# A fused attention and mixture-of-experts kernel: SyncE's registers choose the tiles' rows in place of VectorE's tables

## The chip, the cores and the metric

The kernel runs on one core of a Trainium2 chip. The metric is the device time of one execution in microseconds; the median of several runs counts, and less is better. The engines are called as the profile calls them: PE is TensorE, DVE is VectorE, ACT is ScalarE, POOL is GpSimd and SP is SyncE, which here issues nearly all plain transfers.

## The reference

There are 8 x 3584 = 28,672 tokens of 192 numbers. The first half is a causal convolution of seven taps with weights of its own for each token and each of eight heads (a softmax over the taps); the second is a layer of eight experts, of which each token goes to one.

```python
w = softmax(weight_gen, axis=-1)                      # (B, S, 8 heads, 7 taps)
x = sum over k of w[b, s, h, k] * x_pad[b, s + k, h]  # 24 numbers to a head
logits = x @ w_gate                                   # 8 experts
e_idx = argmax(logits); gate_w = softmax(logits)[e_idx]
eom = sigmoid(x @ w_output_gate)[e_idx]
out = gate_w * eom * (relu(x @ w1[e_idx]) @ w2[e_idx])   # 192 -> 1024 -> 192
```

## The kernel before

**Units.** The tokens are worked in 32 units of 896 (128 partitions by seven). For each unit VectorE and GpSimd make the softmax and the seven products (`softmax_steps`, L544; `tap_steps`, L577); in the first seven units TensorE adds the products in PSUM, later VectorE does (`acc_steps`, L612). `sum_steps` (L680) writes the sum as two 16-bit halves into a tile `rt`; seven DMA transposes, issued by SyncE, turn it (`gt`), and TensorE makes the gate logits. VectorE finds each token's expert and a running count; two small matmuls (L762) give, for each expert, the tokens on the partitions before and the unit's total. `place_steps` (L835) turns them into a row number for each token, and GpSimd scatters the tokens with seven indirect DMAs (`srtd<-rt,posi`) into `srtd`, a tensor in HBM in which each expert has a region of 2^15 rows. The total becomes the next unit's `base`.

**Tiles.** The expert layer works on tiles of T = 512, 384, 256 or 128 rows of one expert. `plan_rounds` (L27) fixes ahead, for each unit, how many tiles of which size follow it: enough rows are held back (`HOLD`, six times T) that some expert always has T rows ready. There are 76 tiles: ten small ones after units 2, 4 and 5 to start with, two more after unit 6, then one or two of 512 a unit, and 23 after the last one. Which expert and which rows a tile takes is known only on the chip. `tile_load` (L1003) reads both into SyncE's registers and issues the tile's loads: the rows' tokens and weights (`meta`), the rows themselves, transposed (`xT`), and the expert's weights in two halves (`wa`, `wb`). `gemm1_unit` and `gemm2_group` (L1018, L1040) are the two matrix products, 40 and 24 matmuls a group of 128 rows; between them ScalarE makes `hh`, the upper half of relu, and VectorE `hl`, the lower, and the PSUM bank is free when `hl` is done (L1038).

**The table.** `round_table` (L878) chooses on VectorE. For a round of R tiles of T rows it compares what each expert has with what the next tiles need, sums up over experts (a scan, L906), and forms from the sums the first row of each tile: `ti[1]` holds the rows, `ti[0]` the experts (a shift by 15, L925). It takes some eight VectorE instructions on one partition, of 8 or 16 elements in most rounds. `tile_load` reads two numbers of it for a tile (`value_load`, L1005 and L1006: a load from SBUF, and a test of its range). The last unit's table is followed by a dozen instructions that count what remains (L949 to L967); a loop behind the 76 tiles would work it off.

**The order of the work.** All engines' instructions stand in one order that a planner makes while the program is built (`Order`, L76): steps are generators, each engine has a clock of modelled costs, and the step that can start earliest goes next; ties go by rank. Each engine carries out its own instructions strictly in that order. A tile's first loads wait for the scatters that `state["writers"]` names (`scattered`, `loaded`, L390 to L403): all that stand ahead of the load in the program. SyncE's instructions (loads, transposes, register loads) stand in one row too, and one that waits holds up those behind it. At most two tiles are loaded ahead of TensorE (`AHEAD`), four after the last unit.

Of the kernel before, what the change touches and what calls it, by code (L numbers as in the profile page):

```python
# [17 lines left out]
P = 128  # L18
W = 194
WW = 3585  # L20
RMAX = 24
SHIFT = 15
NE = 8
# [32 lines left out]
def constants():  # L56

    ident = np.eye(P, dtype=np.float32)
    upper = np.triu(np.ones((P, P), np.float32), 1)
    r = np.arange(RMAX, dtype=np.float32)  # L60
    rr = np.tile(r[:, None], (1, 9))
    need = [T * r for T in (128, 256, 384, 512)]
    e8 = np.arange(8, dtype=np.float32) - 8.0
    flat = np.concatenate([rr.ravel(), *need, e8]).astype(np.float32)
    return np.concatenate([ident, upper, np.tile(flat[None], (P, 1))], axis=1)
# [41 lines left out]
class Queue:  # L107
# [110 lines left out]
def kernel(ctx: ExitStack, tc: tile.TileContext, x, wg, wgate, wogate, w1, w2, cst, out):  # L218
# [69 lines left out]
    f_mx = few[:, 80:136]  # L288
    f_lim = few[0:1, 189:190]

    f_next = few[0:1, 136:152].rearrange("p (e r) -> p e r", r=2)
    f_z = few[0:1, 152:170].rearrange("p (e r) -> p e r", r=2)
    f_done = f_next[:, :, 0]
    f_ex = ps[:, 2536:2538].bitcast(I32)
    f_rr = ps[0:1, 2512 : 2512 + RMAX]

    rest_free = [(0.0, 3904), (0.0, 1344)]
    mx_free, few_free, sq_free = [0.0], [0.0], [0.0]
# [44 lines left out]
    cf = cp.tile([P, cst.shape[1]], F32, name="cf")  # L343
    nc.scalar.dma_start(out=cf, in_=cst)
# [14 lines left out]
    o = 256  # L359
    rr = cf[0:1, o : o + RMAX * 9].rearrange("p (a b) -> p a b", b=9)  # L360
    o += RMAX * 9
    need = {}
    for k in (128, 256, 384, 512):
        need[k] = cf[0:1, o : o + RMAX]
        o += RMAX
    nc.vector.tensor_copy(f_e8, cf[:, o : o + 8])
# [3 lines left out]
    for e in range(NE):  # L370
        nc.vector.memset(base[:, e : e + 1], float(e * CAP - 1))
        nc.vector.memset(f_done[:, e : e + 1], float(e * CAP))


    cs = cp.tile([1, 1 + 8 * RMAX], F32, name="cs")
    nc.vector.memset(cs[:, 0:1], 0.0)
    nc.vector.memset(f_z[:, 8, :], float(DUMMY))
    nc.vector.tensor_copy(f_rr, rr[:, :, 0])
# [9 lines left out]
    state = {"base": base, "writers": [], "t": 0, "weights": 0, "rounds": 0}  # L388

# [154 lines left out]
    def softmax_steps(u):  # L544

        w4 = wloads[u]
        mxb = f_mx.unsqueeze(2).broadcast_to([P, NV, K])
        yield from take(mx_free, V)
# [21 lines left out]
        mx_free.append(od.cur.t)  # L570
# [109 lines left out]
    def sum_steps(u):  # L680
# [84 lines left out]
        od.add(place_steps(u), (RANK_C, u, 0), V)  # L765

# [67 lines left out]

    def place_steps(u):  # L835
# [11 lines left out]
        d["rk_home"].append((od.cur.t, d["rk_at"]))  # L847
        d["ranked"] = True
        if u in plan:
            od.add(round_steps(u), (RANK_R, u), V)  # L850
        else:
            state["rounds"] += 1
# [20 lines left out]
        d["sent"] = True  # L873
        d["sent_t"] = od.cur.t + 2.5
        rt_free.append((d["sent_t"], d["ri"]))


    def round_table(r, T, R, tail, bs):  # L878

        nm = f"{r}"  # L880
        rT = need[T][:, 0:R].unsqueeze(1).broadcast_to([1, 8, R])
        if R > 2:
            n = R
            nx = sp.tile([1, 8, RMAX], F32, tag="nx", bufs=1, name=f"nx{nm}")[:, :, 0:R]
            z = sp.tile([1, 9, RMAX], F32, tag="z", bufs=1, name=f"z{nm}")[:, :, 0:R]
            V.memset(z[:, 8, :], float(DUMMY))
            V.tensor_tensor(out=nx, in0=f_done.unsqueeze(2).broadcast_to([1, 8, R]), in1=rT, op=ALU.add)
            state["step"] = None
            yield V
        else:  # L890
            if state.get("step") != T:
                state["step"] = T if R == 2 else None
                if R == 2:
                    V.tensor_scalar(f_next[:, :, 1], f_done, float(T), None, op0=ALU.add)
                    yield V
            n = 2 if state["step"] == T else 1
            nx, z = f_next[:, :, 0:n], f_z[:, :, 0:n]

        gg = sp.tile([1, 8 * RMAX], F32, tag="gg", bufs=1, name=f"gg{nm}")[:, 0 : 8 * R]
        V.scalar_tensor_tensor(out=gg.rearrange("p (e r) -> p e r", r=R), in0=bs[0:1, :].unsqueeze(2).broadcast_to([1, 8, R]), scalar=0.0 if tail else 1.0 - T, in1=nx[:, :, 0:R], op0=ALU.add, op1=ALU.is_ge)  # L900
        yield V

        if state.get("limit") != R:
            V.memset(f_lim, float(R))
            state["limit"] = R
        V.tensor_tensor_scan(out=cs[:, 1 : 1 + 8 * R], data0=gg, data1=f_lim.broadcast_to([1, 8 * R]), initial=0.0, op0=ALU.add, op1=ALU.min)  # L906
        yield V
        cx = cs[:, 0 : 1 + 8 * R : R]

        V.scalar_tensor_tensor(out=z[:, 0:8, :], in0=cx[:, 0:8].unsqueeze(2).broadcast_to([1, 8, n]), scalar=-float(T), in1=nx, op0=ALU.mult, op1=ALU.add)  # L910
        ge = sp.tile([1, RMAX, 9], F32, tag="ge", bufs=1, name=f"ge{nm}")[:, 0:R, :]
        V.tensor_tensor(out=ge, in0=cx.unsqueeze(1).broadcast_to([1, R, 9]), in1=f_rr[:, 0:R].unsqueeze(2).broadcast_to([1, R, 9]), op=ALU.is_le)
        yield V
        n = 1 if R > 2 else n
        V.scalar_tensor_tensor(out=f_next[:, :, 0:n], in0=cx[:, 1:9].unsqueeze(2).broadcast_to([1, 8, n]), scalar=float(T), in1=z[:, 0:8, 0:n], op0=ALU.mult, op1=ALU.add)
        V.tensor_tensor(out=ge, in0=ge, in1=z[:, :, 0:R].rearrange("p e r -> p r e"), op=ALU.mult)
        yield V
        if R > 8:
            ti = sp.tile([1, 2, RMAX], I32, tag="til", bufs=1, name=f"ti{nm}")
        else:  # L920
            ti = sp.tile([1, 2, 8], I32, tag="ti", bufs=NU // 2 + 6, name=f"ti{nm}")
        with nc.allow_low_precision(reason="whole numbers"):
            V.tensor_reduce(out=ti[:, 1, 0:R], in_=ge, axis=AX, op=ALU.max)
        yield V
        V.tensor_scalar(ti[:, 0, 0:R], ti[:, 1, 0:R], SHIFT, None, op0=ALU.arith_shift_right)  # L925
        yield V
        return ti
# [3 lines left out]
    def round_steps(u):  # L931

        found, bs = [], U[u]["base"]
        yield V, lambda: state["rounds"] == u
        for k, (T, R) in enumerate(plan[u]):
            tail = u == NU - 1 and k == len(plan[u]) - 1
            pads = None
            if tail:
                pads = sp.tile([1, NE], I32, tag="bi", name="bi")
                bf = sp.tile([1, NE], F32, tag="bf", name="bf")  # L940
                V.tensor_scalar(bf, bs[0:1, :], 1.0, None, op0=ALU.add)
                yield V
                V.tensor_copy(pads, bf)
            ti = yield from round_table(f"{u}_{k}", T, R, tail, bs)
            for i in range(R):
                found.append((T, ti, i, pads if i == 0 else None))
        if u == NU - 1:

            more = sp.tile([1, NE], F32, tag="more", bufs=1, name="more")  # L949
            state["done"] = cp.tile([1, NE], F32, name="done")  # L950
            V.tensor_copy(state["done"], f_done)
            V.tensor_tensor(out=more, in0=bs[0:1, :], in1=f_done, op=ALU.subtract)
            yield V
            V.tensor_scalar(more, more, 128.0, None, op0=ALU.add)
            yield V
            morei = sp.tile([1, NE], I32, tag="morei", bufs=1, name="morei")
            V.tensor_copy(morei, more)
            yield V
            V.tensor_scalar(morei, morei, 7, None, op0=ALU.arith_shift_right)
            yield V  # L960
            V.tensor_copy(more, morei)
            yield V
            left = sp.tile([1, 1], F32, tag="left", bufs=1, name="left")
            V.tensor_reduce(out=left, in_=more, axis=AX, op=ALU.add)
            yield V
            lefti = state["left"] = sp.tile([1, 1], I32, tag="lefti", bufs=1, name="lefti")
            V.tensor_copy(lefti, left)  # L967
        state["rounds"] += 1
        yield SP, has(u, "sent")
        queue.extend((*f, max(od.cur.t, U[u]["sent_t"])) for f in found)  # L970
        if u == NU - 1:
            state["all"] = True
            queue[:] = mixed(queue)
# [8 lines left out]
    def tile_steps():  # L982

        while "all" not in state or queue:
# [4 lines left out]
            T, ti, i, pads, ready = queue.pop(0)  # L989
# [3 lines left out]
            if pads is not None:  # L993
                for e in range(NE):
# [308 lines left out]
```

## Time and profile before

| | us |
|---|---|
| median of 3 runs | 1228.21 |
| lowest and highest run | 1226.5, 1228.29 |
| the profiled execution's own time | 1230.08 |
| its span, first to last instruction | 1228.0 |

| engine | busy us | share of the span |
|---|---|---|
| TensorE, matmuls | 1132.9 | 92% |
| VectorE | 956.4 | 78% |
| GpSimd | 879.8 | 72% |
| ScalarE | 594.5 | 48% |

The shares are means over stretches that differ: the experts' weights are split into halves first, then units and tiles go side by side until the last unit, and the rest is tiles alone. Every instruction that the planner places bears the line of its helper (L151, or L125 for SyncE's and GpSimd's queues), so a row is known by its tiles. "x <- y" names what is written and what is read. In a row of waits stand the engine, what it was about to write, what it waited for, the total in us, how many times, and the longest. Waits belong to instructions in order: an engine that waits may hold back something else that was ready.

### The profile page before, as it was taken

To read this page: it belongs to the slowest core of one execution; us is meant where nothing else is said; L and a number is where in the kernel's file an instruction comes from. 1 tells how busy PE (TensorE), PEld (TensorE's weight loads), DVE (VectorE), ACT (ScalarE), POOL (GpSimd) and SP (SyncE) were. 2 spreads that over 40 slices of the span, in tenths; PEclk is the share of its full clock that TensorE was granted. 3 is DMA by queue.
4 is the path that set the end of the run, shared out by engine and by line. 5 is a ranking of instruction groups with operands and counts; after the bars stand their busy time and mean duration, and the time that the engine had idled before them with its cause. 6 is when DMAs were issued, how large, how long until landed. Compare 5 with 4: busy or idle time off the path is not lost.

```text
span 1228.0 us, 27900 instructions
## 1 busy us (share of the span) xinstructions
PE 1132.9 (92%) x9710; PEld 821.3 (67%) x9710; DVE 956.4 (78%) x2027; ACT 594.5 (48%) x1263; POOL 879.8 (72%) x778
## 2 busy tenths in 40 slices
PE   5988779899999999899999999899998999999997
PEld 2444448677666666676766666676666777988987
DVE  6898759899999898998998999899998663333331
ACT  3875345455555445454544454445544544344342
POOL 5668786668888788888888988888887663322222
PEclk9998989899999999999999999999999999999999
DMA  9998378999989869698769759997777679889992
GB/s 281 284 283 288 131 237 196 262 277 250 247 232 240 206 182 248 150 262 211 213 191 229 208 154 244 231 234 188 207 203 185 178 219 278 235 255 330 272 310 80
DMA packets 278047, 279.73 MB, mean 228 GB/s; under 512 B 211479, under 2 KB 236808, under 8 KB 277905
## 3 DMA queue, kind: packets, MB, share of 16 engines
q1 hardware_dynamic: 256016, 233.35, 69.1%
q0 software_dynamic: 21744, 44.30, 13.3%
q8 instruction: 76, 1.25, 0.4%
q14 instruction: 67, 0.54, 0.1%
q10 hardware_dynamic: 144, 0.29, 0.1%
HBM read 177.07 MB, written 60.87 MB: 194 GB/s over the span
## 4 chain that ended last, share of the span: by engine, by line
PE 40%; DVE 26%; POOL 12%; issue 8%; DMA 7%; SPq 3%; ACT 3%; POOLq 0%; DVEq 0%; ACTq 0%
PE ps L151 40%; DVE ps L151 11%; POOL gap L151 6%; DVE hl L151 5%; POOL srtd L151 3%; SPq L125 3%; DMA srtd<-rt,posi 2%; POOL out_dram L151 2%; DMA wa<-wd 2%; DVE rt L151 2%; DMA gt<-rt 1%; DVE vap L151 1%; ACT rt L151 1%; DVE ti L151 1%; DVE vt L151 1%
## 5 line engine op out<-in xcount | busy, mean ns | idle before, releaser
L151 PE MATMUL ps<-xT,wa 128*128 128x512 f16 (+3 forms) x2440 | 493.0, 350 | 42.7 <-DVE hl L151 33.3
L151 PE MATMUL ps<-wb,hh 128*128 128x192 f16 x3664 | 478.9, 248 | 4.8 <-DVE hl L151 4.8
L151 PE MATMUL ps<-wb,hl 128*128 128x192 f16 x1832 | 454.1, 248 | 0.1
L151 DVE SCALAR_TENSOR_TENSOR hl<-ps,hh 128x512 f16<-128x512 f32 (+1 forms) x472 | 307.5, 665 | 156.3 <-ACT hh L151 155.9
L151 POOL TENSOR_TENSOR gap<-x,w 128x960 f32<-128x960 f32 (+5 forms) x268 | 360.0, 1368 | 37.1 <-DVE lz L151 9.2
L151 ACT ACTIVATE hh<-ps 128x512 f16<-128x512 f32 (+1 forms) x472 | 272.1, 582 | 226.1 <-PE ps L151 223.5
L151 PEld LDWEIGHTS <-wa 128*128 128x128 f16 x2440 | 226.5, 99 | 226.7 <-issue 48.8
L151 PEld LDWEIGHTS <-hh 128*128 128x128 f16 x3664 | 337.0, 99 | 50.5 <-issue 9.4
L151 POOL DMA_INDIRECT out_dram<-ys,meta x216 | 214.5, 993 | 193.6 <-ACT ys L151 146.3
L151 POOL DMA_INDIRECT srtd<-rt,posi x224 | 229.0, 1022 | 87.0 <-issue 56.4
L151 DVE TENSOR_TENSOR ps<-ps,gap 128x1344 f32<-128x1344 f32 x125 | 194.2, 1554 | 21.8 <-POOL gap L151 21.8
L151 ACT ACTIVATE ys<-ps,sc 128x192 f32<-128x192 f32 x229 | 96.3, 421 | 221.0 <-PE ps L151 160.5
L151 PEld LDWEIGHTS <-hl 128*128 128x128 f16 x1832 | 180.9, 99 | 0.6 <-DVE hl L151 0.3
L151 PE MATMUL ps<-gap,cf 128*128 128x512 f32 x168 | 72.9, 569 | 3.2 <-DVE vap L151 3.2
L151 PE MATMUL ps<-vap,cf 128*128 128x512 f32 (+1 forms) x126 | 58.2, 603 | 13.5 <-DVE vap L151 12.9
L151 POOL TENSOR_TENSOR gap<-halo,w 128x1152 f32<-128x1152 f32 (+4 forms) x38 | 60.4, 1589 | 13.2 <-issue 5.7
L151 DVE SCALAR_TENSOR_TENSOR rt<-ps,sx,rt 128x448 f16<-128x448 f32 x64 | 57.9, 908 | 10.4 <-ACT rt L151 5.8
L151 PE MATMUL ps<-xT,late 128*128 128x128 f16 (+2 forms) x600 | 56.6, 251 | 0.0
L151 ACT ACTIVATE rt<-ps 128x1344 bf16<-128x1344 f32 x32 | 41.3, 1291 | 28.2 <-issue 18.3
L151 PEld LDWEIGHTS ps<-gap,cf 128*128 128x128 f32 x168 | 31.4, 199 | 34.8 <-issue 25.6
L151 PEld LDWEIGHTS ps<-vap,cf 128*128 128x128 f32 x126 | 24.9, 208 | 38.7 <-issue 22.9
L151 ACT ACTIVATE rt<-ps,sx 128x1344 f16<-128x1344 f32 x32 | 44.2, 1380 | 9.6 <-DVE isx L151 7.6
(123 smaller groups left out, 841.8 us busy)
## 6 DMA issues: line engine op xcount, KB each, us to landing
wb<-wd SPq DMA_DIRECT2D x76, 768.5 KB
wa<-wd SPq DMA_DIRECT2D x61, 768.0 KB
x<-in_x_dram SPq DMA_DIRECT2D x32, 672.0 KB
late<-wd SPq DMA_DIRECT2D x15, 768.0 KB
wa<-wd SPq DMA_DIRECT2D x61, 128.0 KB
w<-in_wg_dram SPq DMA_DIRECT2D x32, 196.0 KB
wd<-wpb SPq DMA_DIRECT2D x8, 768.5 KB
st<-in_w_dram SPq DMA_DIRECT2D x8, 768.0 KB
```

Source lines behind the costliest of these rows:

```text
L125: r = f(*args, **kwargs)
L151: r = f(*args, **kwargs)
```

## The change

The expert and row of a tile are chosen by SyncE's own register arithmetic.

- Each expert has a register `key`: what it has ready, times 2^11, plus its next free row divided by 128. ScalarE copies a unit's eight totals from PSUM into SBUF as whole numbers times 2^11 (`count_steps`); SyncE loads all eight in one load and adds them to the keys (`counted`).
- `pick` takes the largest key, or an unused row if none has T rows, and moves that key on: a start, eight maxima, three operations for each expert, and a mask. That is 34 register operations a tile. `tile_load` takes expert and row from the result; it loads nothing from SBUF.
- A unit's choices are made when its counts have come, ahead of its scatters; its tiles go into the queue when the scatters are issued, as before.
- With each unit the list of the scatters so far is kept (`writers`), and a tile's loads wait for its own unit's list.
- The last unit's pad rows are written when it is chosen for (`end_of`), and the number of leftover turns is made in registers and fetched from a constant table (`turns_left`).
- The softmax has two sets of words in PSUM (`mx_free`) where it had one.
- The constants' transfer shrinks from 576 columns to 264. The tables' VectorE instructions are gone.

The core of the diff:

```diff
-    mx_free, few_free, sq_free = [0.0], [0.0], [0.0]
+    mx_free, few_free, sq_free = [(0.0, 80), (0.0, 136)], [0.0], [0.0]
...
+    def spend(self, us):
+
+        self.issued = max(self.issued, self.order.now) + us
...
-    nc.scalar.dma_start(out=cf, in_=cst)
+    nc.scalar.dma_start(out=cf, in_=cst[:, 0:264])
...
+    def counted(cnt):
+
+        R.reg_load(came, cnt[0:1, 0:NE])
+        for e in range(NE):
+            R.reg_alu(key[e], key[e], came[e], ALU.add)
+        SP.spend(0.6)
+
+    def pick(T):
+
+        R.reg_mov(best, (T - 1 << HAVE) + (DUMMY >> ROW))
+        for e in range(NE):
+            R.reg_alu(best, best, key[e], ALU.max)
+        for e in range(NE):
+            R.reg_alu(came[e], key[e], best, ALU.is_ge)
+            R.reg_alu(came[e], came[e], (T >> ROW) - (T << HAVE), ALU.mult)
+            R.reg_alu(key[e], key[e], came[e], ALU.add)
+        R.reg_alu(best, best, low, ALU.bitwise_and)
+        SP.spend(1.1)
+        return R.snap(best, min_val=0, max_val=DUMMY >> ROW)
+
+    def end_of(e):
+
+        R.reg_alu(hit, key[e], HAVE, ALU.arith_shift_right)
+        R.reg_alu(best, key[e], low, ALU.bitwise_and)
+        R.reg_alu(best, best, 1 << ROW, ALU.mult)
+        R.reg_alu(best, best, hit, ALU.add)
+        row = R.snap(best, min_val=0, max_val=DUMMY - P)
+        scattered(SP.dma_start(out=srtd[bass.ds(row, P), :], in_=pad))
+        R.reg_alu(key[e], key[e], P - 1 << HAVE, ALU.add)
...
+    def count_steps(u):
+
+        cnt = U[u]["cnt"] = sp.tile([1, NE], I32, tag="cnt", bufs=CNT, name=f"cnt{u}")
+        S.activation(cnt, U[u]["rk"][0:1, 8:16], AF.Copy, scale=float(1 << HAVE))
...
+        d["writers"] = list(state["writers"])
...
-    def round_table(r, T, R, tail, bs):
...
     def round_steps(u):
 
-        found, bs = [], U[u]["base"]
-        yield V, lambda: state["rounds"] == u
...
+        yield SP, lambda: state["rounds"] == u and "counted" in U[u]
+        od.cur.t = max(od.cur.t, U[u]["counted"])
+        yield SP
+        counted(U[u]["cnt"])
+        found, subs = [], [(T, k) for k, (T, n) in enumerate(plan.get(u, ())) for _ in range(n)]
+        for T, k in subs:
+            if u == NU - 1 and k == len(plan[u]) - 1 and "ended" not in state:
+                state["ended"] = True
+                for e in range(NE):
+                    yield SP
+                    end_of(e)
+                    od.cur.t = od.now
+            yield SP
+            found.append((T, pick(T), u))
+        state["rounds"] += 1
...
-            d = tile_load(state["t"], T, ti, i, list(state["writers"]), ka, kb)
+            d = tile_load(state["t"], T, at, U[u]["writers"], ka, kb)
...
-    def tile_load(t, T, ti, i, writers, ka, kb):
+    def tile_load(t, T, at, writers, ka, kb):
         Gn = T // P
-        e = SP.value_load(ti[0:1, 0, i : i + 1], min_val=0, max_val=NE - 1)
-        row = SP.value_load(ti[0:1, 1, i : i + 1], min_val=0, max_val=DUMMY + 4 * P - T)
+        R.reg_alu(hit, at, SHIFT - ROW, ALU.logical_shift_right)
+        e = R.snap(hit, min_val=0, max_val=NE - 1)
+        row = at * (1 << ROW)
```

More of the change, by code (lines that the diff above doesn't have):

```diff
@@ L59, in constants @@
     upper = np.triu(np.ones((P, P), np.float32), 1)
-    r = np.arange(RMAX, dtype=np.float32)
-    rr = np.tile(r[:, None], (1, 9))
-    need = [T * r for T in (128, 256, 384, 512)]
     e8 = np.arange(8, dtype=np.float32) - 8.0
-    flat = np.concatenate([rr.ravel(), *need, e8]).astype(np.float32)
+    turns = np.arange(TURNS, dtype=np.int32).view(np.float32)
+    flat = np.concatenate([e8, turns])
     return np.concatenate([ident, upper, np.tile(flat[None], (P, 1))], axis=1)
@@ L371 @@
         nc.vector.memset(base[:, e : e + 1], float(e * CAP - 1))
[L372 to L378, printed above, removed]
+    R = nc.sync
+    key = [R.alloc_register(f"key{e}") for e in range(NE)]
+    came = [R.alloc_register(f"came{e}") for e in range(NE)]
+    best, hit = R.alloc_register("best"), R.alloc_register("hit")
+    for e in range(NE):
+        R.reg_mov(key[e], e << SHIFT - ROW)
     pad = cp.tile([P, W], I32, name="pad")
@@ L873, in place_steps @@
         d["sent"] = True
+        d["writers"] = list(state["writers"])
         d["sent_t"] = od.cur.t + 2.5
         rt_free.append((d["sent_t"], d["ri"]))
-    def round_table(r, T, R, tail, bs):
[L880 to L927, printed above, removed]
@@ L929 @@
     queue = []
     def round_steps(u):
-        found, bs = [], U[u]["base"]
-        yield V, lambda: state["rounds"] == u
[L935 to L946, printed above, removed]
@@ L947, in round_steps @@
-        if u == NU - 1:
[L949 to L967, printed above, removed]
@@ L988, in tile_steps @@
             _, kb = yield from take(wb_free, SP)
-            T, ti, i, pads, ready = queue.pop(0)
+            T, at, u, ready = queue.pop(0)
             if ready > od.now:
@@ L992, in tile_steps @@
                 yield SP
-            if pads is not None:
-                for e in range(NE):
-                    row = SP.value_load(pads[0:1, e : e + 1], min_val=0, max_val=DUMMY - P)
-                    scattered(SP.dma_start(out=srtd[bass.ds(row, P), :], in_=pad))
-            d = tile_load(state["t"], T, ti, i, list(state["writers"]), ka, kb)
+            d = tile_load(state["t"], T, at, U[u]["writers"], ka, kb)
             d["ready"] = od.cur.t
@@ L1202 @@
     own.close()
-    left = nc.values_load(state["left"][0:1, 0:1], min_val=0, max_val=N // P + NE)
+    lefti = cp.tile([1, 1], F32, name="lefti")
+    nc.sync.dma_start(out=lefti, in_=cst[0:1, bass.ds(state["turns"] + 264, 1)])
+    left = nc.values_load(lefti.bitcast(I32)[0:1, 0:1], min_val=0, max_val=TURNS - 1)
     gps.close()
@@ L1209 @@
         _, more = wa_free.pop()
[L1210 to L1216 removed]
+        d = tile_load(state["t"], P, pick(P), [], more, "wb")
         state["t"] += 1
@@ L1280 @@
 GT = 1
+CNT = 4
 TR_U = 6
```

61 lines of the change are left out of this document (30 added, 31 removed).

## The prediction

> **What bounds the kernel now.** I read the page first, then the busy time in four stretches, then the waits of each engine in those stretches, and last the chain and the timelines around TensorE's longest gaps. From the page:
>
> ```profile
> span 1228.0 us, 27900 instructions
> ```
>
> ```profile
> PE 40%; DVE 26%; POOL 12%; issue 8%; DMA 7%; SPq 3%; ACT 3%; POOLq 0%; DVEq 0%; ACTq 0%
> ```
>
> The chain passes mostly through TensorE and VectorE, with little on the transfers and on SyncE (SPq). The four stretches (weights are split; the first tiles; units and tiles side by side; tiles alone) give busy time per engine:
>
> ```profile
> 0.00:175.00 175.00, 139.82 (x580) 72.11 (x581) 131.81 (x303) 98.43 (x165) 124.88 (x104) 0.95 0.81 251
> 175.00:250.00 75.00, 62.96 (x584) 52.44 (x583) 63.68 (x149) 36.84 (x87) 50.89 (x42) 0.87 0.92 235
> 250.00:963.00 713.00, 672.82 (x5817) 481.50 (x5815) 665.42 (x1385) 351.35 (x788) 612.83 (x537) 0.98 0.83 215
> 963.00:1228.00 265.00, 257.33 (x2734) 215.29 (x2733) 95.49 (x194) 107.83 (x225) 91.23 (x96) 1.00 0.84 244
> ```
>
> The columns behind the length are PE, PEld, DVE, ACT and POOL. After 963 us TensorE works off the queue of tiles with nothing in its way. So the end is set by TensorE's work, which the change leaves alone, plus TensorE's idle time before 963: 713 - 673 = 40 us in the third stretch and 75 - 63 = 12 us in the second. That idle time is what can be won or lost. What ends it, in the second stretch and shortly before it (140 to 250 us, first row) and in the third (other two):
>
> ```profile
> PE ps L151 <- DMA wa<-wd: 8.1, 2, 5.9
> ```
>
> ```profile
> PE ps L151 <- DVE hl L151: 34.4, 38, 2.6
> PE ps L151 <- DMA gt<-rt: 4.5, 9, 0.8
> ```
>
> (us in total, times, longest). TensorE waits for VectorE's hl, which frees its PSUM banks; for the transposes gt of the gate logits; and early for two weight loads. In the third stretch VectorE, GpSimd and SyncE wait in their turn:
>
> ```profile
> DVE ps L151 <- POOL gap L151: 21.8, 18, 2.4
> ```
>
> ```profile
> POOL srtd L151 <- issue: 43.6, 146, 0.3
> POOL out_dram L151 <- issue: 20.3, 95, 0.3
> ```
>
> ```profile
> SPq L125 <- DMA srtd<-rt,posi: 128.6, 34, 10.4
> SPq L125 <- DVE rt L151: 63.1, 13, 15.2
> ```
>
> GpSimd's 612.8 busy plus 63.9 of short pauses ahead of its indirect DMAs is 676.7 of 713 us, so the units come at GpSimd's pace; VectorE (665.4) is close behind. SyncE stands still 128.6 us for scatters into the sorted rows.
>
> **The change part by part.**
>
> *VectorE's tables go.* The third stretch has these groups, among others (busy us, mean ns):
>
> ```profile
> L151 DVE TENSOR_SCALAR ti<-ti 1x2 int32<-1x2 int32 x17 | 17.9, 1053 | 0.0
> ```
>
> ```profile
> L151 DVE SCALAR_TENSOR_TENSOR ps<-cs,ps 1x16 f32<-1x16 f32 x44 | 7.3, 166 | 1.2
> ```
>
> ```profile
> L151 DVE TENSOR_SCALAR ti<-ti 1x1 int32<-1x1 int32 x7 | 0.9, 132 | 0.0
> ```
>
> These rows alone are 17.9 + 7.3 + 0.9 = 26.1 us in 24 tables (17 of two tiles, 7 of one); a table has five steps more, at the 166 ns of the second row 24 x 5 x 0.166 = 20 us, so I put it at some 45 us. Most is off the path: it is work of an engine that waits for GpSimd anyway. What lies on the path is the shift that makes ti: 132 ns for one element but a mean of 1053 for two, so some of them stand still for microseconds. The chain names three (start, us), and TensorE's waits in the stretches right behind them (503 to 507, 691 to 699, 872 to 880 us) follow:
>
> ```profile
> 500.93 3.29 DVE ti L151
> ```
>
> ```profile
> 691.67 3.07 DVE ti L151
> ```
>
> ```profile
> 872.74 2.44 DVE ti L151
> ```
>
> ```profile
> PE ps L151 <- DVE hl L151: 2.6, 1, 2.6
> ```
>
> ```profile
> PE ps L151 <- DVE hl L151: 2.6, 1, 2.6
> ```
>
> ```profile
> PE ps L151 <- DVE hl L151: 0.8, 1, 0.8
> ```
>
> The hl that TensorE needs stands behind the shift on VectorE. Without the shift 2.6 + 2.6 + 0.8 = **6.0 us** go; what is late next there is the sum of GpSimd's products that follows the shift. Bounds: nothing, if the stall only passes to the next VectorE operation, to all 6.0. I take 6.0, since the stall shows on this operation and not on its neighbours of a table (166 ns). The Trainium skill (SBUF — State Buffer, "Who interferes with whom") says that a tensor_scalar can run in a mode that needs the port pair shared with GpSimd, and that the later of the two then waits for the other's whole instruction. By that rule the stall belongs to the shift, and leaves with it; the other reading, that any operation in that place would stall, makes this term 0.
>
> *A tile waits for its own unit's scatters alone.* Before, a tile's first load waits for every scatter that is written ahead of it in the program, newer units' too. At 198.7 us SyncE is done with a store; the next load, of a tile of unit 4, starts at 205.35, and unit 4's last scatter had been issued at 179.17 (the later ones are unit 5's). TensorE's wait in 205 to 216 us is the last row:
>
> ```profile
> 198.71 0.36 SPq L125 DMA_DIRECT2D yd<-ys  x1
> 205.35 0.40 SPq L125 DMA_DIRECT2D meta<-srtd  x1
> ```
>
> ```profile
> 179.17 1.02 POOL L151 DMA_INDIRECT srtd<-rt,posi  x1 [0.17 <-issue]
> ```
>
> ```profile
> PE ps L151 <- DMA wa<-wd: 2.2, 1, 2.2
> ```
>
> SyncE could go on some 6 us sooner, which covers the 2.2: **-2.2 us** (bounds 0 to -8.1, both early weight loads; the other, 5.9, follows a run of transposes on SyncE, so I leave it). In the third stretch the 128.6 us are mostly hidden, for TensorE waits for no tile there. They cost where transposes stand behind them. At 768.43 SyncE issues an x load, then nothing until 779.34; the transposes come at 783.56, and TensorE's wait in 780 to 800 is the last row:
>
> ```profile
> 768.43 0.36 SPq L125 DMA_DIRECT2D x<-in_x_dram  x1
> 779.34 0.41 SPq L125 DMA_DIRECT2D meta<-srtd  x1
> ```
>
> ```profile
> 783.56 11.82 SPq L125 DMA_TRANSPOSE gt<-rt  x7
> ```
>
> ```profile
> PE ps L151 <- DMA gt<-rt: 2.6, 5, 0.8
> ```
>
> I take **-2.6 us** (bounds 0 to -4.5, all waits for gt). SyncE's 63.1 us for VectorE's rt stay: there the transposes themselves are early.
>
> *VectorE has time to spare.* Of the 34.4 us for hl, 6.0 are taken above. Much of the rest follows a wait of VectorE for GpSimd's products; in 415 to 420 us, for one:
>
> ```profile
> DVE ps L151 <- POOL gap L151: 1.5, 1, 1.5
> ```
>
> ```profile
> PE ps L151 <- DVE hl L151: 2.0, 1, 2.0
> ```
>
> A lighter VectorE does not shorten these, for GpSimd's work is as before. Of the remaining 28.4 us I take **-2 us**, nearest to the share that the removed work has of VectorE's (45 of 665, 7%). Bounds: -11, if the waits that follow no wait for GpSimd go, up to +22 (a rival below).
>
> *SyncE's registers.* A choice is 34 register operations, and each unit has one load of eight counts and eight additions. Rows of SyncE (min/median/max ns):
>
> ```profile
> L125 SPq FUSED_REGOPS  x548: 37/51/178, 141.8 to 1194.9; - x183
> ```
>
> ```profile
> L125 SPq TENSOR_LOAD <-ti x152: 261/278/935, 141.1 to 1190.5; - x152
> ```
>
> At 51 ns each a choice is 34 x 0.051 = 1.7 us if every operation is an instruction of its own, about 0.6 us if three go into one, 6.1 us at the longest 178. It takes the place of two loads with their range tests, 2 x (0.28 + 0.05 to 0.18) = 0.7 to 0.9 us. At 1.7 this is +0.9 us for each tile, and 0.28 + 8 x 0.05 = 0.7 us for each unit: with 1.75 tiles to a unit, 2.3 us more of SyncE's time. The cover is SyncE's own waits, (128.6 + 63.1)/24 = 8.0 us to a unit. So I cost it at 0 (bounds 0 to +20, a rival). The Trainium skill (Perfetto Trace Analysis, "Sequencer-only Instruction (DRAIN, etc)") says that the profile shows only the execution of such an instruction, not its decoding, waiting or semaphore push. By that rule a choice costs more than its rows add up to; were it twice, 3.4 us, the unit's addition would be 5.3 us, an estimate, and still under the cover.
>
> The load of counts waits for ScalarE, in order: behind it stand the next x and w loads, the transposes and the tiles' loads, and through them GpSimd and TensorE. It stands where the counts are planned to be there, ahead of the unit's scatters, for the last of which SyncE waits today. ScalarE gets 32 copies of eight counts; the nearest row is
>
> ```profile
> L151 ACT ACTIVATE rt<-tok 128x14 int32<-128x14 f32 x32 | 6.7, 210 | 3.9 <-DMA srtd<-rt,posi 3.9
> ```
>
> so 32 x 0.21 = 6.7 us on an engine that is idle half the time; but each waits for TensorE's count with TensorE's next hh behind it. **+1 us** (bounds 0 to +6.7).
>
> *The rest.* Two softmax word sets let a unit's softmax begin before the former's weights are done; nothing on TensorE's list waits for that: 0 (bounds -2 to +2). The constants' load shrinks to less than half; VectorE's first copy waits for it
>
> ```profile
> DVE ps L366 <- DMA cf<-in_cst_dram: 4.7, 1, 4.7
> ```
>
> beside the first weights and products, which are later: **-0.5 us** (bounds -2 to 0). The eight pad rows and the count of leftover turns move within the stretch in which TensorE has a queue: 0.
>
> **Sum.** -6.0 - 2.2 - 2.6 - 2 + 1 - 0.5 = -12.3 us. The profiled execution took 1230.08 us, its span of 1228.0 and 2.1 around it, so 1217.8 by its own time. The median of the runs, 1228.21, is 1.9 lower: 1215.9, and I say **1216**.
>
> **The rivals.**
>
> *GpSimd is the pace and VectorE runs into it (slower).* VectorE, lighter by 45 us, comes sooner to each sum and waits there for GpSimd's product with the hl behind it. For it: 1.5 us of such a wait went with 2.0 us lost on TensorE, and GpSimd has only 713 - 677 = 36 us to give. Against it: the order is one of planned times, and a VectorE that comes early to a sum comes early to the hl ahead of it too. If half of the 45 us turns into such waits and TensorE pays each in full, it is +22 + 2 (the term taken for relief) - 12.3 = +12, or 1240. It decides from 12 us of added waits.
>
> *SyncE becomes late (slower).* Place: the last unit, whose 23 choices and eight pads follow each other before the next tile's load. At 1.7 us they are 39 us. Two tiles are loaded ahead; a tile is 713/((5817 - 24 x 23)/136) = 18.4 us of TensorE (136 matmuls to a tile of 512, 23 small ones to a unit), so 37 us are covered, and more than half a tile under way. At twice the price, 78 us, TensorE would stand some 30 us: +30 - 12.3, about 1246. It decides where the choices outlast the cover of 46 us by 12.3, from 58/23 = 2.5 us a choice.
>
> *The gaps move (same).* The places named are 11 us of 52; if what is late next there is as late, the end stays: 1226 to 1230. The 5.9 us wait that I left speaks for it, as do the sums of GpSimd behind each shift.
>
> *The front speeds up (faster still).* With SyncE free of 129 us of waits and the scatters' gate weights no longer behind the shift, GpSimd gives up its 36 us, the third stretch is shorter by that, and its 40 us of gaps shrink by half: -20 - 5, about 1203.
>
> *It doesn't do what it says:* most scatters waited for might be the tile's own unit's, and SyncE stand as before. Then -2.2 and -2.6 fail: 1221, within the forecast's range.
>
> **How the numbers follow.** The forecast (terms as above, 1206 to 1224) has 0.58; the faster rival 0.14; the same 0.11; VectorE against GpSimd 0.10; SyncE late 0.07. A difference under 0.2% (2.5 us) is no change. Faster 0.58 + 0.14 = 0.72, same 0.11, slower 0.17. The range goes down to 1200, which leaves out about half of the faster rival, and up to 1237, which leaves out about half of the slower ones.
>
> **What would show it.** Right: no ti group on VectorE, whose busy time between 250 us and the end of the units falls by about 45 us; no VectorE operation on one partition of several us; TensorE's wait for hl under 28 us; SyncE's wait for scatters well under 60 us, with waits for ScalarE's counts in its place; TensorE's early wait for wa at about 6 us. Wrong: VectorE's wait for GpSimd's products over 35 us with hl at 40 or more (first rival); a gap on TensorE near 1000 us that a weight load ends (second); the same 50 us of gaps in other places (third); units ending well before 950 us (fourth).

## The result, and the profile after

| | before | after |
|---|---|---|
| median of 4 runs, us | 1228.25 | 1271.97 |
| lowest and highest run | 1226.5, 1228.31 | 1267.03, 1274.07 |
| span of the profiled execution | 1228.0 | 1268.9 |

After is slower: the ratio is 1.0354 (95% interval 1.0321 to 1.0386), 43.7 us. The forecast was 1216, with 1200 to 1237 as its range, and its direction was wrong.

From the page of after, the span and the chain of work that ended last, by engine:

```profile
span 1268.9 us, 27805 instructions
```

```profile
PE 43%; POOL 17%; DVE 12%; issue 10%; DMA 10%; SPq 4%; ACT 2%; POOLq 0%; DVEq 0%; ACTq 0%
```

GpSimd and the transfers have taken VectorE's place on the chain. Where the 40.9 us of span are is seen when both executions are cut at the same times. First before, then after (length, then busy PE, PEld, DVE, ACT, POOL, the granted clock, DMA share, GB/s):

```profile
0.00:250.00 250.00, 202.78 (x1162) 124.55 (x1163) 195.50 (x451) 135.27 (x252) 175.76 (x146) 0.92 0.84 246
250.00:950.00 700.00, 660.19 (x5713) 472.58 (x5711) 654.22 (x1352) 345.52 (x772) 601.43 (x527) 0.98 0.83 216
950.00:1228.00 278.00, 269.96 (x2838) 224.22 (x2837) 106.68 (x226) 113.66 (x240) 102.63 (x106) 1.00 0.82 240
```

```profile
0.00:250.00 250.00, 204.33 (x1218) 126.80 (x1219) 197.61 (x410) 140.16 (x270) 180.21 (x152) 0.94 0.84 248
250.00:950.00 700.00, 633.73 (x5416) 452.05 (x5415) 606.59 (x1143) 335.50 (x765) 595.49 (x521) 0.96 0.78 210
950.00:1268.90 318.90, 301.70 (x3082) 245.72 (x3080) 102.43 (x169) 122.06 (x261) 101.93 (x107) 0.98 0.76 220
```

TensorE's idle time in the middle goes from 39.8 to 66.3 us (+26.5), after 950 us from 8.0 to 17.2 (+9.2), ahead of 250 us from 47.2 to 45.7 (-1.5). Its busy time grows by 6.8 us for the same matmuls, at a lower granted clock (0.962 for 0.974 over the whole span). That is the whole 40.9, to rounding. VectorE is lighter by 48 us in the middle, as the prediction had it, and the ti group is gone.

The waits between 250 and 950 us, of TensorE and of VectorE, in before:

```profile
PE ps L151 <- DVE hl L151: 34.0, 37, 2.6
DVE ps L151 <- POOL gap L151: 20.7, 17, 2.4
```

and in after:

```profile
PE ps L155 <- DVE hl L155: 44.1, 38, 6.7
PE ps L155 <- ACT cnt L155: 5.6, 4, 3.0
```

```profile
DVE ps L155 <- POOL gap L155: 39.9, 32, 3.1
DVE ps L155 <- DMA w<-in_wg_dram: 34.0, 8, 7.0
```

TensorE's wait for hl rose although VectorE has less to do. VectorE now stands still 34 us for the softmax's own input `w`, for which it did not wait before, and 39.9 us for GpSimd's products (19 us more than before). One of the waits for `w`, in the timelines of SyncE, VectorE and TensorE:

```profile
321.16 0.37 SPq L129 DMA_DIRECT2D w<-in_wg_dram  x1
```

```profile
321.82 0.57 DVE L155 TENSOR_REDUCE ps<-w 128x56 f32<-128x392 f32 x1
322.43 0.56 DVE L155 TENSOR_TENSOR w<-w,ps 128x392 f32<-128x392 f32 x1
329.94 0.57 DVE L155 TENSOR_REDUCE ps<-w 128x56 f32<-128x392 f32 x1 [6.96 <-DMA w<-in_wg_dram]
330.45 0.68 DVE L155 SCALAR_TENSOR_TENSOR rt<-ps,sx,rt 128x448 f16<-128x448 f32 x1
331.05 1.01 DVE L155 SCALAR_TENSOR_TENSOR hl<-ps,hh 128x384 f16<-128x384 f32 x2
```

```profile
331.65 2.29 PE L155 MATMUL ps<-xT,wa 128*128 128x512 f16 x5 [6.65 <-DVE hl L155]
```

One unit's softmax begins at 321.82 with its maximum and its difference. With a second set of words the next unit's may begin before that one is through, and the planner puts its maximum (329.94) right behind; its difference follows only at 358.8, so nothing needs the maximum that early. Its `w` was asked for only at 321.16 and is there at 329.9, 8.8 us later; at all eight such waits it was there 5.4 to 8.8 us after it was asked for. The planner reckons with 2.2 us on a free queue (`sync_cost`: 200,704 bytes at 360 a ns are 0.56, and `Queue` adds 0.65 and 1.0). VectorE stands in order, the hl behind it is late, and TensorE loses 6.65 us. Behind seven of the eight waits a wait of TensorE ends within 3 us of VectorE's, 26.9 us together. That is as much as its idle time in the middle grew, though not all of it need be the load's doing.

The other place is the last unit. SyncE's rows there (min/median/max ns, first and last start), its timeline, and TensorE's next wait:

```profile
L394 SPq FUSED_REGOPS  x23: 185/185/195, 980.8 to 1015.3; - x23
```

```profile
979.50 0.40 SPq L129 DMA_DIRECT2D wb<-wd  x1
996.32 6.13 SPq L129 DMA_DIRECT2D srtd<-pad  x8
1018.10 0.42 SPq L129 DMA_DIRECT2D meta<-srtd  x1
1018.69 1.61 SPq L129 DMA_TRANSPOSE xT<-srtd  x1
1020.56 0.36 SPq L129 DMA_DIRECT2D wa<-wd  x1
```

```profile
1026.62 2.74 PE L155 MATMUL ps<-xT,wa 128*128 128x512 f16 x6 [9.71 <-DMA wa<-wd]
```

The 23 choices and eight pads stand in one row, from 980.8 to past 1015.3 us, and no tile is loaded meanwhile. TensorE has used up the tiles loaded ahead at 1016.9 and stands 9.71 us.

### The profile page after: what moved, and what is told of

It is laid out like the page before. It is cut to its first block, busy times and chain, and to the rows that moved or that the text cites. A ratio compares the mean times of both kernels' runs of the same rounds, so it can differ in the third digit from the quotient of the medians.

```text
span 1268.9 us, 27805 instructions
## 1 busy us (share of the span) xinstructions
PE 1139.8 (90%) x9710; PEld 824.6 (65%) x9710; DVE 906.6 (71%) x1721; ACT 597.7 (47%) x1295; POOL 877.6 (69%) x778
## 4 chain that ended last, share of the span: by engine, by line
PE 43%; POOL 17%; DVE 12%; issue 10%; DMA 10%; SPq 4%; ACT 2%; POOLq 0%; DVEq 0%; ACTq 0%
PE ps L155 43%; POOL gap L155 9%; DVE ps L155 5%; POOL srtd L155 4%; DMA w<-in_wg_dram 4%; POOL out_dram L155 4%; DVE hl L155 2%; DMA srtd<-rt,posi 2%; SPq L129 2%; DMA wa<-wd 2%; DMA x<-in_x_dram 1%; DVE vap L155 1%; ACT hh L155 1%; DMA st<-in_w_dram 1%; DVE rt L155 1%
## 5 line engine op out<-in xcount | busy, mean ns | idle before, releaser
L155 PE MATMUL ps<-xT,wa 128*128 128x512 f16 (+3 forms) x2400 | 480.8, 349 | 64.7 <-DVE hl L155 41.1
L155 PEld LDWEIGHTS <-wa 128*128 128x128 f16 x2400 | 222.2, 99 | 242.8 <-issue 64.3
L155 POOL DMA_INDIRECT srtd<-rt,posi x224 | 225.8, 1008 | 91.3 <-issue 59.8
L155 DVE TENSOR_TENSOR ps<-ps,gap 128x1344 f32<-128x1344 f32 x125 | 194.9, 1559 | 40.5 <-POOL gap L155 39.9
L155 PE MATMUL ps<-xT,late 128*128 128x128 f16 (+2 forms) x640 | 72.8, 269 | 0.0
L155 DVE TENSOR_REDUCE ps<-w 128x56 f32<-128x392 f32 x64 | 36.2, 566 | 38.5 <-DMA w<-in_wg_dram 36.3
L155 PEld LDWEIGHTS <-late 128*128 128x128 f16 x640 | 47.8, 98 | 16.3
L155 ACT ACTIVATE rt<-ps,sx 128x1344 f16<-128x1344 f32 x32 | 44.1, 1379 | 19.9 <-DVE isx L155 16.1
```

Source lines behind the costliest of these rows:

```text
L155: r = f(*args, **kwargs)
```

## The experiments

Four theories. **A**: the second softmax set costs, since the plan puts a softmax ahead of its load's landing. **B**: the load of the counts, which waits in order for ScalarE, holds up SyncE's loads. **C**: the last unit's choices stand ahead of tiles that TensorE needs. **D**: a lighter VectorE comes early to GpSimd's products and pays there (the prediction's first rival).

The first four kernels ran on a chip on which before took 1228.20. After was not run again beside them; its 1271.97 is from the runs above, where before took 1228.25, and differences to it are taken on that ground. The other fourteen ran on four other chips, on which before itself took 1288 to 1296 us. A ratio is always to before on the same chip. The two kinds of chip are set side by side only where that is said.

### The first chip: one part undone at a time

**One softmax set in after** (A):

```
-    mx_free, few_free, sq_free = [(0.0, 80), (0.0, 136)], [0.0], [0.0]
+    mx_free, few_free, sq_free = [(0.0, 80)], [0.0], [0.0]
```

> The changed kernel with one softmax word set, as before. Theory A (the second set lets a unit's softmax stand on VectorE right behind the planned landing of its weights, so VectorE waits there for the load, 34 us between 250 and 950 us): VectorE's wait for w falls under 5 us, TensorE's idle time falls by 20 us or more, the time to about 1250. Theory B (SyncE issues the weights' loads late, since the load of counts holds it up): VectorE's wait for w stays over 20 us and the time over 1264.

Measured: 1249.24, ratio 1.0166 (1.0130 to 1.0203); 22.7 us of the loss go. VectorE's waits in the middle:

```profile
DVE ps L155 <- POOL gap L155: 47.3, 29, 4.5
DVE ps L155 <- DMA w<-in_wg_dram: 3.4, 2, 1.8
```

The wait for `w` falls from 34.0 to 3.4 us, and TensorE's idle time in the middle by 15.3, short of the 20 that were the mark:

```profile
250.00:950.00 700.00, 649.00 (x5598) 462.91 (x5595) 614.11 (x1163) 345.51 (x793) 603.37 (x531) 0.98 0.80 215
```

Over the whole span, 21.5 us shorter, TensorE has 10.9 us less idle time and 10.6 less busy time (1129.2 for 1139.8) at a granted clock of 0.971 for 0.962. The waits for gap are higher still, so they are not what the second set made.

**Two sets in before**, tables kept (what the second set's room needs of PSUM is moved):

```
-    mx_free, few_free, sq_free = [0.0], [0.0], [0.0]
+    mx_free, few_free, sq_free = [(0.0, 80), (0.0, 136)], [0.0], [0.0]
...
+        _, mx_at = yield from take(mx_free, V)
+        f_mx = few[:, mx_at : mx_at + NV]
```

> The kernel before with a second softmax word set and nothing else (its tables' words move to other places in PSUM, and the tables' rows are cut to 12). Theory A: VectorE waits 20 us or more for w loads, as in the changed kernel, and the time is 1245 or more. Theory B: VectorE waits for w under 5 us, since SyncE loads no counts here, and the time stays within 5 us of 1228.

Measured: 1228.21, ratio 0.9989 (0.9970 to 1.0008), with

```profile
DVE ps L151 <- DMA w<-in_wg_dram: 10.4, 5, 3.7
```

So the second set alone costs no time, and theory A in its plain form fails. But the same waits are there in small: behind three of the five TensorE stands 7.2 us, and its idle time in the middle is 47.3 us in place of 39.8, made up for by 6.3 us less of busy time, for a reason not known. What costs 22.7 us is the set together with the rest of the change, whose plan moves the softmax close to its load more often (8 such waits, 34.0 us, for 5). Why it does was not taken apart.

**The last unit's choices behind the tiles** (C), an order of ranks:

```
-        od.add(round_steps(u), (RANK_R, u), SP)
+        od.add(round_steps(u), (RANK_R, u) if u < NU - 1 else (RANK_A, 0), SP)
```

> The changed kernel with the last unit's choices ranked behind the tiles' loads on SyncE. Theory C (the 37 us run of choices and pad rows on SyncE near 980 us delays one tile's loads, and TensorE stands 9.7 us and then runs at a lower clock): the gap near 1017 us shrinks to under 2 us and the time falls by 8 to 14, to about 1260. Rival (the tile would have waited anyway, for the last scatters): the gap stays within 3 us of 9.7 and the time within 4.

Measured: 1257.98, ratio 1.0243 (1.0207 to 1.0278); 14.0 us go. No wait of TensorE is listed after 950 us, and its idle time there is 306.3 - 299.0 = 7.3 us in place of 17.2:

```profile
950.00:1256.30 306.30, 299.02 (x3077) 245.00 (x3074) 102.14 (x165) 122.72 (x260) 101.68 (x106) 0.99 0.79 229
```

**Counts and choices only behind a unit's scatters** (B): `round_steps` waits for `has(u, "sent")` before `counted`.

> The changed kernel with a unit's counts loaded and its tiles chosen only once its scatters are issued, not ahead of them. Theory B: SyncE's waits for ScalarE at the load of counts (36 us between 250 and 950 us) go, the w loads come sooner, VectorE's wait for w falls under 15 us and the time by 15 us or more. Theory A: the waits for counts go, but VectorE's wait for w stays over 20 us and the time within 8 us of 1272.

Measured: 1274.68, ratio 1.0367 (1.0321 to 1.0414), no better than after. SyncE's waits at the load of the counts, in the middle, fall from 36 to 5 us as meant, but VectorE still waits for `w`:

```profile
DVE ps L155 <- DMA w<-in_wg_dram: 30.4, 7, 6.1
```

B falls: the count loads' waits are covered.

### The slower chips: parts together

| kernel | ratio to before (95% interval) |
|---|---|
| after | 1.0073 (1.0037 to 1.0108) |
| after, w planned to land 7 us later | 1.0011 (0.9985 to 1.0037) |
| that, last unit's choices behind the tiles | 0.9916 (0.9882 to 0.9950), 0.9928 (0.9897 to 0.9958), 0.9908 (0.9878 to 0.9938), 0.9900 (0.9869 to 0.9932) |
| that, a tile waiting for all scatters | 0.9901 (0.9867 to 0.9934) |
| one set, last unit's choices behind the tiles | 1.0005 (0.9984 to 1.0025), 1.0009 (0.9978 to 1.0039), 0.9990 (0.9966 to 1.0015) |
| that, VectorE's load put back | 1.0013 (0.9990 to 1.0036) |
| before, own unit's scatters alone | 1.0005 (0.9972 to 1.0037) |
| before, one delay of the plan 1.1 for 1.0 us | 1.0051 (1.0021 to 1.0081) |
| before, two sets, w planned 7 us later | 1.0081 (1.0056 to 1.0106) |

**Both undone, the landing planned, VectorE's load put back, the order nudged.** The edits:

```
             w_load(u)
-            U[u]["wt"] = od.cur.t
+            U[u]["wt"] = od.cur.t + 7.0
```

```
+    def table_steps(u):
+        yield V, has(u, "ranked")
+        for k in range(9):
+            V.scalar_tensor_tensor(out=du, in0=du, scalar=0.0, in1=ds, op0=ALU.mult, op1=ALU.add)
+            yield V
...
+        if u in plan:
+            od.add(table_steps(u), (RANK_R, u), V)
```

```
-LAT_R = 1.0
+LAT_R = 1.1
```

> After with two edits together: one softmax word set, and the last unit's choices ranked behind the tiles. Theory A+C (the two costs are separate places): 1272 - 22.7 - 14 = about 1235, VectorE's wait for the w load under 5 us and no TensorE gap over 5 us after 950 us. If the two overlap (both only shift the same idle time): 1244 or more. If these two are the whole loss and the gains that were forecast are there as well: 1216 to 1225.

> After with two sets kept, the last unit's choices behind the tiles, and the plan told that a w load is there 7 us later than it reckons now (the softmax is put that much later into VectorE's order). Theory A (the second set costs because the softmax is ordered ahead of its load's landing): as the kernel with one set, within 4 us of it, with VectorE's wait for w under 12 us. Rival (the second set costs through something else, such as softmax work ahead of TensorE's hl): no better than the kernel with the last unit's choices moved alone, 1255 to 1260.

> One set, the last unit's choices behind the tiles, and beside them nine unused VectorE operations of 1x16 for each unit with tiles, as many as a table had (they are planned as the tables were; the shift is left out). About 9 x 0.166 = 1.5 us a unit, some 45 us of VectorE. Theory D (a lighter VectorE comes early to GpSimd's products, and the order planned for it costs): faster than the kernel without them by 4 us or more, VectorE's wait for gap back towards 22 us. Rival (the waits for gap come from elsewhere): the same within 2 us, or slower by up to 10.

> Before, with one delay of its plan at 1.1 in place of 1.0 us (the wait from a unit's ranks to their product on TensorE): nothing of the work changes, only the order that comes out of the plan. It shows how far a mere reordering moves the time. If the order is robust: 1226 to 1231. If any other order is some per cent worse, 1240 or more, then part of the loss of after is that its plan is not tuned again.

The times expected were for the first chip; here the ratios count. With one set and the last unit mended the change is as fast as before (1288.47 beside 1288.93). With two sets and the later landing it is faster (1277.21), 11.3 us from the kernel with one set, where theory A had the two within 4. VectorE's load put back (38 us of busy time, measured) changes nothing beyond the noise (1290.55 beside 1288.47), where D asked for 4 us less, so D falls there; a relief of 2 us, as forecast, can be neither seen nor excluded. An order changed for no reason at all costs half a per cent, so differences of about that size between two plans need not have a cause in what was edited.

**After itself beside single edits.**

> After unchanged, as the measure for the three kernels beside it. The four kernels before these ran on a chip on which the kernel before itself took 1289 us, not 1228, so that their ratios cannot be set beside those of the first four. If the loss is one of the order alone, its ratio is 1.035 here too; on a chip as slow as that of the last four it could differ by a per cent or more.

> After with two sets and the last unit's choices where after has them; the one edit is that the plan reckons each w load as landed 7 us later. Theory A (the second set costs because the plan puts a softmax ahead of its load's landing): as much faster than after as one set alone was, 1.7 to 2%, with VectorE's wait for w under 12 us. Rival (the second set costs in another way): under 0.7%.

> Both edits: the later landing and the last unit's choices behind the tiles. Theory A+C: the sum of the two, 3% under after, about the time of before. If the gains that were forecast are there beneath the two losses: under before by some 0.5 to 1%, as on the slow chip (0.9916). Rival (something else in the change costs as well, such as the waits for gap): over before by 0.5% or more.

> One set and the last unit's choices behind the tiles, beside the three above. Theory A+C: 3% under after, within 1% of before. If the second set, once its landing is planned rightly, brings what it was made for: slower than the kernel with two sets and the later landing by 0.3 to 1%; if it brings nothing, the two are the same.

After loses 0.7% here, not 3.5%. Its wait for `w` is less than half of that on the first chip, first row; the landing alone takes off 0.6 points and leaves no such wait on VectorE's list, and the gap after 950 us remains, second row (of the kernel with that edit alone); the last unit's order takes off 0.8 more. The 0.6 points are most of what there was to win, but they lie under the 0.7 that was set as the rival's mark, and are no more than a nudged order makes. So the landing is shown here by the wait, and not by the time, and on the first chip the later landing was not run.

```profile
DVE ps L155 <- DMA w<-in_wg_dram: 14.8, 5, 4.8
```

```profile
PE ps L155 <- DMA wa<-wd: 13.0, 1, 13.0
```

Two sets with the later landing are 0.8 points faster than one set without it (0.9928 to 1.0009, and again 0.9908 to 0.9990 on another chip). One set with the later landing was not run, so what the set and the landing each give is not told apart.

**A tile's own writers**, alone in before and taken back in the best kernel:

```
-            d = tile_load(state["t"], T, ti, i, list(state["writers"]), ka, kb)
+            d = tile_load(state["t"], T, ti, i, U[u]["writers"] if u < NU - 1 else list(state["writers"]), ka, kb)
```

```
-            d = tile_load(state["t"], T, at, U[u]["writers"], ka, kb)
+            d = tile_load(state["t"], T, at, list(state["writers"]), ka, kb)
```

> Later landing of w in the plan and the last unit's choices behind the tiles, as the kernel that was 0.7% under before on the slower chip. Theory A+C (those two are the loss): on any chip under before, 0.992 to 0.996; 1218 to 1224 where before takes 1228. Rival (another cost of the change shows where the chip is fast, the waits for GpSimd's products): 1.005 or more there.

> One set and the last unit's choices behind the tiles, beside the kernel before. Theory A+C: 0.5 to 1 point above the kernel with two sets and a later landing, as on the slower chip (1.0009 to 0.9928). If the second set brings nothing: the same.

> Before with one part of the change alone: a tile waits for the scatters up to its own unit's last, not for all issued so far. By the forecast's terms -2.2 and -2.6: 4.8 us less, a ratio of 0.996. Rival (what SyncE waited for is hidden or is late anyway): within 0.2% of before.

> The kernel with the later landing and the last unit after, in which a tile again waits for all scatters issued so far. By the forecast's terms 4.8 us or 0.4 points slower than that kernel, with SyncE's wait for srtd between 250 and 950 us higher by 30 us or more. Rival: the same within 0.2%.

Neither edit moves the time beyond the noise (1.0005, and 0.9901 beside 0.9908). SyncE's wait for scatters in the middle is not longer with all writers (second row) than with a tile's own (first):

```profile
SPq L129 <- DMA srtd<-rt,posi: 87.6, 20, 9.5
```

```profile
SPq L129 <- DMA srtd<-rt,posi: 83.3, 26, 8.9
```

**Tables beside registers**, with the same two sets and the same landing:

> Later landing of w in the plan and the last unit's choices behind the tiles, beside the kernel with tables below. On a chip where before takes 1285 to 1295: 0.991 to 0.993 as in three calls. Where before takes 1228, theory A+C says under 1.0, 1218 to 1226; the rival (waits for GpSimd's products cost there) says 1.005 or more.

> Before, tables on VectorE and all, with the second softmax set and w loads planned as landed 7 us later. If the choices on SyncE bring the gain: within 0.3% of before, so 0.5 points or more over the kernel beside it. If the planned landing with the second set brings it: 0.991 to 0.995, the same as the kernel beside it within 0.2 points.

The kernel with registers took 1283.27, the one with tables 1307.29: 0.9900 to 1.0081. So the gain is not that of the planned landing alone; before with it is slower. Busy time in the middle, registers and then tables:

```profile
250.00:950.00 700.00, 640.62 (x5529) 455.95 (x5530) 616.71 (x1155) 335.22 (x780) 598.03 (x522) 0.98 0.80 212
```

```profile
250.00:950.00 700.00, 625.72 (x5261) 440.23 (x5262) 608.74 (x1253) 315.74 (x715) 549.36 (x482) 0.97 0.77 203
```

By 950 us the kernel with registers has done 268 matmuls more, about two tiles, and 49 us more of GpSimd's work. Which part makes this (the shift, the tables' place in VectorE's order, the wait of SyncE for their result, or the order that came out of the plan, nudged by the landing) was not taken apart. GpSimd's lag alone need not cost: with VectorE's load put back, above, it had done 21 us less by 950, and the time stayed.

## Why the prediction was wrong, point by point

**"Two softmax word sets ... 0 (bounds -2 to +2)"** is the step that failed most: undoing it gave 22.7 us on the first chip. The reason given was that nothing on TensorE's list waits for a softmax. But a softmax stands in VectorE's order ahead of hl, and the planner puts it there by a landing of 2.2 us where 5.4 to 8.8 were measured. In the middle, VectorE's list of before has no wait for `w`: with one set each softmax stays behind the former's end, and with two sets in before waits for `w` of 10.4 us appear. The edit removed that hidden guard; this cost no time in before, and 22.7 us in the plan of after. The prediction did not ask what the wait that goes had been keeping apart.

**"The eight pad rows and the count of leftover turns ...: 0"** failed too, and the rival for SyncE at the last unit had the mechanism and the place. It asked for 2.5 us a choice before it decides. A choice took (1015.3 - 980.8 - 6.1)/22 = 1.3 us, less than the 1.7 taken, and still TensorE stood. What was mis-sized is the cover of 46 us: from the last load, at 979.50, TensorE's loaded tiles held out 37.4 us, to 1016.9, and the next tile's weights landed only some 6 us after they were asked for at 1020.56. Choices and pads, 37 us, filled all of that cover; the transposed load and the landing came on top. Moving them behind the tiles gave 14.0 us, forecast as nothing.

The Trainium skill (Perfetto Trace Analysis, "Sequencer-only Instruction (DRAIN, etc)") says that decoding and waiting of such instructions are not shown. A choice's rows are 29 to 245 ns each, under 1 us together by the rows of its lines, and choices follow each other every 1.3 us, so some time is indeed unseen: about a third of what the rows show, and not the doubling that the prediction weighed.

**The shift, -6.0.** The ti group is gone, and in after no short instruction of VectorE takes over its stall: the one-column int32 shift that every unit still has (`ex_x`) stays short.

```profile
L155 DVE TENSOR_SCALAR ex_x<-ssq x32: 127/148/154, 31.9 to 947.1; 128x1 int32<-128x1 int32 x32
```

So the stall belonged to that instruction, as forecast. What its going is worth in time was not measured by itself.

**A tile's own writers, -2.2 and -2.6.** Nothing, on the slower chips: in before the ratio was 1.0005 (0.9972 to 1.0037), and 4.8 us would have been 0.996. In after SyncE still waits 105 us for scatters in the middle (118 in before), where "well under 60" was the mark:

```profile
SPq L129 <- DMA srtd<-rt,posi: 105.0, 30, 11.9
```

That fits scatters that are mostly the tile's own unit's, as the rival "it doesn't do what it says" had it for these terms.

**VectorE's relief, -2, and the rival against GpSimd.** The relief is too small to measure. The rival's sign in the profile was there (gap 39.9, over its mark of 35, hl 44.1, over its mark of 40), but the waits for gap rose to 47.3 in the kernel that was 22.7 us faster, and putting the work back gave nothing on the slower chip. These waits were not shown to be a cause.

**ScalarE's counts, +1.** TensorE's waits for them were 5.6 us, near the upper bound of 6.7, but 5.0 of these come right behind VectorE's waits for `w`: ScalarE's copies of the counts waited there for `base`, which VectorE makes. The kernel with one set lists none. So the term by itself was not seen. SyncE's registers in the units cost nothing that a later choice would win back, as forecast.

**What stays open.** Undone one at a time on the first chip, the two causes are 36.7 of 43.7 us. No kernel with both undone ran there; the 7.0 us left, and the forecast gain, cannot be placed on that chip. On the slower chips the later landing and the last unit's order give the forecast's size, 0.7 to 1.0% under before. That is no proof of the forecast's terms: of these the writers' gave nothing there, VectorE's relief could not be seen, and the shift's was not measured by itself.

## What to carry to other kernels

A buffer that keeps two steps apart may be the only thing that hides a wrong duration in the plan: before giving a second one, look up when the load behind the step lands, and put the measured time into the plan. Such a fault can be there without showing in the time, as with two sets in before. A row of work on a queue is covered only up to the time at which the next load must be issued, so the load's own landing is taken off the cover; work that nobody awaits goes behind what somebody does. And after such a change the plan is a new one: an order merely nudged cost 0.5% on a slower chip.

## What the runs showed of the hardware

The chips differ more than the change: before takes 1228 us on one and 1288 to 1296 on four others, and the loss of after is 3.5% on the first and 0.7% on a slower one. On a slower chip TensorE has waits that no event of the trace releases, in before with a tile's own writers

```profile
PE ps L151 <- issue: 41.5, 56, 4.8
```

while the first chip's list for before has none of that kind for its matmuls. What makes them is not known.

The long waits cost TensorE more than their length here. Five matmuls of one form took 1.24 us behind a wait of 0.96 us, the row below, and 2.29 behind the one of 6.65 us; the granted clock was 1.00 from 318 to 322 us and 0.50 from 331.6 to 335.6. That fits after's 6.8 us more of busy time.

```profile
323.76 1.24 PE L155 MATMUL ps<-xT,wa 128*128 128x512 f16 x5 [0.96 <-ACT ys L155]
```

One load of eight counts into registers takes over twice a load of one number (278 ns, in the prediction's row):

```profile
L385 SPq TENSOR_LOAD <-cnt x32: 533/646/1512, 71.8 to 980.0; - x32
```
